# Attention values padded and packed in DRAM, the last normalisations on VectorE, and earlier filter tables in a four-layer attention and spectral kernel

## The chip, the cores and the metric

The kernel runs on one core of a Trainium2 chip. The metric is device microseconds from start to end of one execution. The kernel before takes 1390.59 us (median of 3 runs, 1387.26 to 1393.25).

## The reference, cut

Four sub-layers work on x, 2048 tokens of 576 values: sliding-window attention, a spectral filter, and both again with the same weights.

```python
def _A_ref(x, wqkv, wo):                 # H = 32 heads, Dh = 18, W = 256
    q, k, v = split of x @ wqkv by heads
    scores = jnp.einsum("bhqd,bhkd->bhqk", q, k) * (Dh ** -0.5)
    mask = (idx[:, None] - idx[None, :] >= 0) & (idx[:, None] - idx[None, :] < W)
    p = _softmax(jnp.where(mask, scores, -1e9), axis=-1)
    o = jnp.einsum("bhqk,bhkd->bhqd", p, v)
    return o.transpose(0, 2, 1, 3).reshape(B, S, D) @ wo

def _B_ref(x, w_r, w_i):
    X = rfft2(x) * (w_r + 1j * w_i)
    return irfft2(X, (S, D))

x = A_x
x = x + _A_ref(_layernorm(x), A_wqkv, A_wo)
x = x + _B_ref(_layernorm(x), B_w_r, B_w_i)
x = x + _A_ref(_layernorm(x), A_wqkv, A_wo)
x = x + _B_ref(_layernorm(x), B_w_r, B_w_i)
```

## The kernel before, in words

`layer_a` is an attention sub-layer, `layer_b` a spectral one. Between them stands the class `Out`, the output projection, whose units of 128 tokens run at once as the end of attention and the start of the spectral layer. TensorE (PE) multiplies, VectorE (DVE), ScalarE (ACT) and GpSimd (POOL) work on tiles, and nearly all transfers are issued by SP, in program order, from one list.

**Attention.** The 32 heads form eight groups (n = 0 to 7) of four. A group has 16 tiles of 128 queries, in four quarters (c) of 512. In a steady state TensorE mixes, in bursts, the work of several stages:

- `proj` (L1091) projects q and k of a later group; they go to DRAM (qk_d, L1126) and come back in a stacked layout by `stack_load` (L1132, 12 transfers of 18 partitions a quarter, L1141). `v_load` (L1144) brings v of a group, `vq` in the trace, 608 KB.
- `score_max` (L1154) multiplies q and k a first time (S, L1166) and VectorE takes each query's maximum (L1168).
- `m_rows` (L1176) turns a quarter's maxima (tile `mt`) and writes them with four small transfers (L1186) into a spare row of q, where k has ones.
- `exps` (L1191) multiplies a second time (E, L1203), now with the maximum subtracted. ScalarE exponentiates (L1204), POOL masks (L1206, L1209).
- `part` (L1214) multiplies by v (U, L1223). A column of ones in v gives the sums. After a quarter VectorE transposes the result (L1228, `us`).
- `divide` (L1236) inverts the sums on VectorE and multiplies on POOL (L1240; VectorE for the last quarter of all), `back` (L1242) transposes on VectorE into `o`, and `store` (L1246) issues four transfers, one a head: the tile has 32 partitions a head, of which 18 hold values, and L1250 stores 18 x 512 each to o_d in DRAM. Group 7's go straight to `out.o7` in SBUF.

The order of SP's list follows the order in which the Python code calls these functions. `bursts` (L1317) does it burst by burst; `later` (L1301) puts divide, back and store 1, 3 and 4 bursts after a quarter's last `part`. From MIX = 118 of 128 tiles a plain loop takes over. `behind` (L1389) interleaves the loads of the output projection: `attended` (L764) reads o_d (`oraw`, in two buffers big(0) and big(1)), `ahead_of_last` (L775) reads the last 56 features of o_d, and `turn` (L778) splits units into a high and a low part, where the subtraction for rows 64 to 127 (L785) is POOL's.

Transfers of SP run under eight semaphores in rotation, so a transfer is issued when the eighth before it has landed.

**Spectral layer.** `pre` (L218) is called once per unit n2 = 0 to 15 and loads the filter tables in eight transfers of 128 x 1024 (512 KB): four of `fc` at n2 = 2, 3, 10, 12 and four of `m2` at 5, 7, 11, 13. Tables 0 lie in big(0) and tables 1 in big(1), the buffers of `oraw`, whose units 0 to 7 and 8 to 15 must be done first. `f4` (L316) stores the units' result `ye` to yd in DRAM, and for the last ones also writes it to SBUF rows `ofree` (L337). In the second spectral layer 29 warm-up matmuls (L374) follow, then the phase `g0`, `g1m`, `g2` (L485 to L571), whose first matmuls (p, L501) read those rows and the tables.

The four transfers of the store:

```python
for h in range(4):
    to = o_d[72 * n + 18 * h:72 * n + 18 * h + 18, c] if n < NQ - 1 else out.o7[18 * h:18 * h + 18, 512 * c:512 * c + 512]
    (engines[h] if engines else nc.sync).dma_start(to, o[32 * h:32 * h + 18])
```

Of the kernel before, what the change touches and what calls it, by code (L numbers as in the profile page):

```python
# [8 lines left out]
F32 = mybir.dt.float32  # L9
# [6 lines left out]
S, D = 2048, 576  # L16
DF = 289
NF = 290
NT = 16
# [117 lines left out]
def layer_b(tc, xf, dst, dcs, gc, ident, rh, rl, big, out, ga_d, fc_d, m2_d, w_d, wo_d, wo2_d, dram, nxt, share):  # L137


    nc = tc.nc  # L140
    V, A, T, P = nc.vector, nc.scalar, nc.tensor, nc.gpsimd
    first = nxt is not None
# [5 lines left out]
    with ExitStack() as stack:  # L148
        banks, inner = ExitStack(), ExitStack()
        ip = stack.enter_context(tc.tile_pool(name="bi", bufs=1))  # L150
        cp = inner.enter_context(tc.tile_pool(name="bc", bufs=1))
# [22 lines left out]
        tables, ets = [], []  # L174
# [12 lines left out]
        for j in range(4):  # L187
            e = (ip if j == 1 else cp).tile([128, 2, 290], F32, name=f"eo{j}")
# [17 lines left out]
        def pre_o(j):  # L206
            nc.sync.dma_start(ws[j][:, 0:D], wo_d[:, j * D:j * D + D])

        def pre_w(k):

            w = wp.tile([128, 2, 2, NF], F32, tag="wt", name=f"wt{k}", bufs=NW)
            nc.sync.dma_start(w.rearrange("p a c f -> p a (c f)"), w_d[2 * k:2 * k + 2].rearrange("a p f -> p a f"))
            for q in range(2):
                wt[2 * k + q] = w[:, q]
# [2 lines left out]

        def pre(n2):  # L218

            if n2 in (2, 10):  # L220
                tables.append(big(n2 // 8, f"tables{n2 // 8}", F32).rearrange("p (w g x) -> p w g x", w=2, g=8))
            for w, d, at in ((0, fc_d, (2, 3, 10, 12)), (1, m2_d, (5, 7, 11, 13))):
                if n2 in at:
                    k = at.index(n2)
                    nc.sync.dma_start(tables[k // 2][:, w, 4 * (k % 2):4 * (k % 2) + 4].rearrange("p g x -> p (g x)"), d[:, 1024 * k:1024 * k + 1024])
            if n2 == 4:
                nc.sync.dma_start(edge[:, 0], fc_d[:, 4096:])
                nc.sync.dma_start(edge[:, 1], m2_d[:, 4096:])
            if n2 % 2 and n2 // 2 < NW:
                pre_w(n2 // 2)  # L230
            if first and n2 in (0, 3, 5, 8, 10):
                pre_o((0, 3, 5, 8, 10).index(n2))
# [83 lines left out]
        def f4(n2, h):  # L316
# [8 lines left out]
            else:  # L325
# [3 lines left out]
                V.tensor_sub(ye[:, 1], pz[:, 0, 0:NF], both[:, 0])  # L329
            yef = ye.rearrange("p j f -> p (j f)")  # L330
            pre(n2)
            if n2 == FD:
                for k in range(1 if first else 2):
# [60 lines left out]
        b = NT - 1  # L394
        if first:
# [24 lines left out]
            for t in range(1, NT - 5):  # L420
                u = t + 4
# [218 lines left out]
NQ = 8  # L640
# [73 lines left out]
class Out:  # L714
# [63 lines left out]
    def turn(self, u, e):  # L778

        raw = self.halves[u // 8].rearrange("p k c (n q) -> p k c n q", q=32)[:, :, :, u % 8]  # L780
        oT = self.oT[u % 3]
        h = oT[:, 0:512].rearrange("p (k c q) -> p k c q", k=4, c=4)
        (self.nc.vector.tensor_copy if e is self.nc.vector else self.nc.scalar.copy)(h, raw)  # L783
        self.nc.vector.tensor_sub(oT[:, 512:896].rearrange("p (k c q) -> p k c q", k=3, c=4), raw[:, 0:3], h[:, 0:3].bitcast(F32))
        self.nc.gpsimd.tensor_sub(h[64:128, 3], raw[64:128, 3], h[64:128, 3].bitcast(F32))  # L785

    def split_last(self, u):

# [73 lines left out]
def layer_a(tc, ident, eps, bp, big, src, dst, wqk_d, wv_d, wo_d, dc_d, gc_d, dram, copy, wvs, second, spectral, share):  # L862

    nc = tc.nc
    V, A, T, P = nc.vector, nc.scalar, nc.tensor, nc.gpsimd
# [2 lines left out]
    v_d = dram.tile([NQ, S, 76] if second else [NQ, 128, NT, 76], F32, name="v_d")  # L868

    o_d = dram.tile([504, 4, 512], F32, name="o_d")  # L870
    r_d = dram.tile([NQ, 4, 4, 512], F32, name="r_d")
    srcv, dstv = [a.rearrange("(p n) e -> p n e", n=NT) for a in (src, dst)]

    tiles = [slice(t * 128, (t + 1) * 128) for t in range(NT)]
# [5 lines left out]
    if True:  # L880
# [191 lines left out]
        with ExitStack() as c2:  # L1072
# [160 lines left out]

            os = {}

            def divide(n, c, drain=False):  # L1236
                u = us[n, c]
                rc = wp.tile([128, NT, 1], F32, tag="rc", name=f"rc{n}_{c}", bufs=2)
                V.reciprocal(rc, u[:, :, 18:19])
                (V if drain else P).tensor_mul(u[:, :, 0:18], u[:, :, 0:18], rc.to_broadcast([128, NT, 18]))  # L1240

            def back(n, c):  # L1242
                os[n, c] = o = wp.tile([128, NT, 32], F32, tag="o", name=f"o{n}_{c}", bufs=2)
                V.transpose(o, us[n, c])

            def store(n, c, engines=None):  # L1246
                o = os[n, c].rearrange("r n p -> r (n p)")
                for h in range(4):
                    to = o_d[72 * n + 18 * h:72 * n + 18 * h + 18, c] if n < NQ - 1 else out.o7[18 * h:18 * h + 18, 512 * c:512 * c + 512]
                    (engines[h] if engines else nc.sync).dma_start(to, o[32 * h:32 * h + 18])  # L1250

            for k, (i, c) in enumerate(((0, 0), (1, 0), (0, 1), (1, 1), (0, 2), (0, 3), (1, 2), (1, 3))):
                for f in proj(i, c, k % 2):
# [45 lines left out]
            steps = {}  # L1299

            def later(k, n, c):  # L1301
                for lag, f in zip(later.lags, (divide, back, store)):
                    steps.setdefault(k + lag, []).append((f, n, c))

            later.lags = 1, 3, 4

# [10 lines left out]
            def bursts():  # L1317
# [63 lines left out]
                for p in parts:  # L1381
                    part(*p)
                    if p[1] and p[0] % 4 == 3:
                        later(k, *divmod(p[0] // 4, 4))

            OB = NX - 8
            out = Out(nc, eps, bp, big, o_d, srcv, dstv, wo_d, dc_d, gc_d, second)

            def behind(t):  # L1389
                if copy and t >= 32 and t % 4 == 0 and t < 32 + 16 * len(copy):  # L1390

                    z, r = divmod(t // 4 - 8, 4)
                    P.dma_start(*[a[32 * r:32 * r + 32] for a in copy[z]])
                if t == OB - 16:
                    out.room()
                if 0 <= t - (OB - 10) < 10 and t % 2 == 0:
                    out.split((t - (OB - 10)) // 2)
                if t - OB + 13 in range(0, 10, 2):
                    out.const((t - OB + 13) // 2)
                if t == OB - 3:  # L1400
                    out.filters()
                if t - OB + 8 in range(0, 10, 2):
                    out.load_x(((t - OB + 8) // 2 + 1) % 5)
                if 0 <= t - (OB - 8) < 6:
                    out.attended(*divmod(t - (OB - 8), 2))
                if t - OB in (1, 2):
                    out.attended(3, t - OB - 1)
                if t == OB + 2:
                    out.ahead_of_last()
                if t - OB - 5 in (0, 1, 2):  # L1410
                    out.turn(t - OB - 5, V)
                if t == NX:

                    A.activation(wp.tile([128, 1], F32, name="se", bufs=1), eps, AF.Sqrt)
# [32 lines left out]
            def bank(tag, name):  # L1447
                return pp.tile([128, 512], F32, tag=tag, name=name, bufs=1 if tag == "pj" else 3)

            out.early(0, [bank(k, f"ops0_{k}") for k in ("pj", "S")], slice(0, 4))  # L1450
            divide(NQ - 1, 3, True)
            back(NQ - 1, 3)
            store(NQ - 1, 3, (nc.sync, nc.scalar, P, nc.sync))
            out.early(0, None, slice(4, 11))
# [56 lines left out]
```

## Time and profile before

| | before |
|---|---|
| median of 3 runs | 1390.59 us (1387.26 to 1393.25) |
| profiled execution, its time | 1393.43 us |
| its span | 1391.4 us |
| mean granted TensorE clock | 0.977 |
| first attention, stores of `o` | 160.9 us on |
| second attention, last store | about 1200 us |
| second spectral layer's warm-up | 1275.33 us |

The span runs from the first to the last instruction. In a timeline a row gives start, duration, engine, line, operation, output <- input, and in brackets how long the engine was idle before it and what ended that. SPq is SP's transfer queue at issue: the duration is that of issuing, not of the transfer. A row of the waits gives the engine and line, what was waited for, us in total, times and the longest. A row of the chain gives start, us and what the end waited for. A row of the windows gives the stretch, its length, busy time (and number of instructions) of PE, PE's weight loads, DVE, ACT and POOL, then the granted clock, the busy share of the 16 DMA engines and GB/s.

### The profile page before, as it was taken

The page shows a single profiled execution, that of the slowest core. Times are in us where ns is not written, and L with a number is a line of the kernel's source. Part 1 is how long each engine was busy: PE and PEld are TensorE (multiplying, and loading weights), DVE is VectorE, ACT ScalarE, POOL GpSimd, SP SyncE. Part 2 cuts the span into 40 slices and gives each one's busy share as a digit, 9 for nine tenths or more (in the row PEclk, how much of TensorE's full clock was granted, in tenths as well). Part 3 has the DMA queues.
Part 4 walks back from the last instruction along what each step waited for, and adds up shares of the span by engine and source line. Part 5 has one row for each costly group of instructions (what it writes and reads, how often), then busy time and mean ns, then how long its engine had stood idle before and what let it go on. Part 6 is the DMA issues. An engine that isn't in the chain of part 4 may idle for free.

```text
span 1391.4 us, 33481 instructions
## 1 busy us (share of the span) xinstructions
PE 1325.8 (95%) x10911; PEld 969.6 (70%) x10911; DVE 943.3 (68%) x3120; ACT 756.4 (54%) x1896; POOL 703.3 (51%) x1168
## 2 busy tenths in 40 slices
PE   9999999999998899999999999999999998998998
PEld 8986556556654499975999975565565554797588
DVE  5418878778887567757673168787788777475855
ACT  5623667567666735543355326676676667574233
POOL 2257556556655734467211395566566557312731
PEclk9999999999999999999999999999999999899999
DMA  6756555554445827678873467455455547488875
GB/s 199 210 168 200 180 169 161 166 170 155 149 143 172 228 72 246 188 247 264 274 246 77 117 200 214 148 163 156 147 155 145 164 130 247 105 291 283 290 242 180
DMA packets 175586, 259.56 MB, mean 187 GB/s; under 512 B 68639, under 2 KB 78623, under 8 KB 174981
## 3 DMA queue, kind: packets, MB, share of 16 engines
q1 hardware_dynamic: 164591, 236.04, 55.3%
q10 hardware_dynamic: 7702, 15.03, 3.1%
q0 software_dynamic: 3120, 6.36, 1.8%
q8 instruction: 88, 1.44, 0.4%
q14 instruction: 85, 0.70, 0.2%
HBM read 156.28 MB, written 100.13 MB: 184 GB/s over the span
## 4 chain that ended last, share of the span: by engine, by line
PE 77%; DMA 11%; DVE 3%; ACT 3%; issue 2%; SPq 2%; POOL 1%; DVEq 0%; ACTq 0%; POOLq 0%
PE pj L1105 18%; PE S L1166 11%; PE U L1223 10%; PE vps L1001 8%; PE ops L798 6%; PE E L1203 6%; DMA qs<-mt 4%; PE po L272 4%; PE p L501 3%; PE pq L522 3%; PE pi L598 2%; PE pf L272 2%; DMA ks<-qk_d 1%; ACT P L1204 1%; DMA qs<-qk_d 1%
## 5 line engine op out<-in xcount | busy, mean ns | idle before, releaser
L1168 DVE CUSTOM_DVE_ANT_0 jk<-S,mask 128x384 bf16<-128x384 f32 (+2 forms) x1024 | 490.3, 526 | 117.7 <-PE S L1166 71.7
L1204 ACT ACTIVATE P<-E 128x384 f32<-128x384 f32 (+2 forms) x1024 | 409.9, 476 | 222.8 <-PE E L1203 176.5
L1166 PE MATMUL S<-ks,qs 63*128 63x384 f32 (+2 forms) x1024 | 284.7, 381 | 1.4 <-DMA qs<-qk_d 0.4
L1206 POOL TENSOR_SCALAR_AFFINE_SELECT P<-P 128x512 f32<-128x512 f32 x256 | 163.3, 638 | 241.5 <-ACT P L1204 235.7
L1203 PE MATMUL E<-qs,ks 64*128 64x384 f32 (+2 forms) x1024 | 240.0, 386 | 36.8 <-DMA qs<-mt 31.7
L1166 PEld LDWEIGHTS S<-ks,qs 63*128 63x128 f32 x1024 | 147.7, 189 | 116.8 <-DVE m L1168 83.6
L1223 PE MATMUL U<-P,vq 128*19 128x128 f32 (+1 forms) x3840 | 197.7, 340 | 3.5 <-DVE us L1228 2.1
L1203 PEld LDWEIGHTS E<-qs,ks 64*128 64x128 f32 x1024 | 122.5, 192 | 61.3 <-issue 31.4
L1223 PEld LDWEIGHTS U<-P,vq 128*19 128x19 f32 x3840 | 98.1, 101 | 88.0 <-issue 27.5
L1105 PE MATMUL pj<-xh,wqh 128*128 128x512 f32 x360 | 158.2, 440 | 0.4 <-DVE sg L1123 0.2
L1209 POOL TENSOR_SCALAR_AFFINE_SELECT P<-P 128x512 f32<-128x512 f32 x224 | 143.3, 640 | 0.0
L1105 PE MATMUL pj<-xh,wql 128*128 128x512 f32 x360 | 122.5, 416 | 0.0
L1105 PE MATMUL pj<-xl,wqh 128*128 128x512 f32 x288 | 121.6, 422 | 0.0
L798 PE MATMUL ops<-oroom 128*128 128x290 f32 (+1 forms) x812 | 114.0, 297 | 1.7 <-DVE ofree L844 1.3
L798 PEld LDWEIGHTS ops<-oroom 128*128 128x128 f32 x812 | 110.4, 189 | 2.3 <-ACT ofree L832 1.5
L1105 PEld LDWEIGHTS pj<-xh,wqh 128*128 128x128 f32 x360 | 68.9, 191 | 33.4 <-issue 15.5
L1168 DVE DVE_READ_ACCUMULATOR2_ANT m<- 128x1 f32 x1024 | 85.5, 84 | 0.0
L1117 ACT CAST sg<-pj 128x512 fp32r<-128x512 f32 x72 | 42.4, 589 | 70.3 <-PE pj L1105 57.8
L1105 PEld LDWEIGHTS pj<-xh,wql 128*128 128x128 f32 x360 | 64.3, 189 | 21.8 <-issue 10.8
L1228 DVE STREAM_TRANSPOSE us<-U 128x512 f32<-128x512 f32 x64 | 45.9, 717 | 44.7 <-PE U L1223 44.7
L785 POOL TENSOR_TENSOR oroom<-oraw,oroom 64x128 fp32r<-64x128 f32 x32 | 17.7, 553 | 100.1 <-ACT oroom L783 56.9
L1105 PEld LDWEIGHTS pj<-xl,wqh 128*128 128x128 f32 x288 | 55.3, 192 | 17.1 <-issue 9.3
(507 smaller groups left out, 2258.1 us busy)
## 6 DMA issues: line engine op xcount, KB each, us to landing
qk_d<-sg SPq DMA_DIRECT2D x56, 512.0 KB
qs<-qk_d SPq DMA_DIRECT2D x384, 72.0 KB
ks<-qk_d SPq DMA_DIRECT2D x348, 72.0 KB
v_d<-vt SPq DMA_DIRECT2D x32, 304.0 KB
vq<-v_d SPq DMA_DIRECT2D x16, 608.0 KB
wt<-in_w SPq DMA_DIRECT2D x16, 580.0 KB
ofree<-x SPq DMA_DIRECT2D x16, 580.0 KB
x<-ofree SPq DMA_DIRECT2D x32, 290.0 KB
```

The costliest lines, as they stand in the source:

```text
L272: T.matmul(ps[:, c, 0:NF], tail[r] if si == 4 else hl_(si), dcs[b // 2][r, b % 2], start=mi == si == 0, stop=si == 4)
L798: self.nc.tensor.matmul(self.ps[u][n][:, 0:self.n], x, self.w[p][:, (2 * wk + n) * self.n:(2 * wk + n + 1) * self.n], start=first and i == ...
L1001: T.matmul(ps[:, n, 0:288], xT(xk, c), w[:, wk, n * 288:(n + 1) * 288], start=i == 0, stop=i == len(ks) - 1)
L1105: T.matmul(box["ps"].rearrange("r (n p) -> r n p", n=NT) if second else box["ps"], w[:, wk], x, start=s == 0, stop=s == len(ks) - 1)
L1166: T.matmul(ps[:, 0:N], q[b:b + 63, pair, i * 128:i * 128 + 128], k[b:b + 63, pair, lo:hi], start=True, stop=True)
L1168: V.tensor_tensor_reduce(out=jk[:, 0:N], in0=ps[:, 0:N], in1=mask[:, 384 - N:384], scale=1.0, scalar=-3e38, op0=ALU.add, op1=ALU.max, accu ...
L1203: T.matmul(ps[:, 0:nq], k[b:b + 64, pair, j * 128:j * 128 + 128], q[b:b + 64, pair, j * 128:j * 128 + nq], start=True, stop=True)
L1204: A.activation(p[:, hl_, 0:nq], ps[:, 0:nq], AF.Exp, scale=SC)
L1206: P.affine_select(out=p[:, :, 0:128], in_=p[:, :, 0:128], pattern=[[0, 4], [1, 128]], compare_op=ALU.is_ge, fill=0.0, base=0, channel_mult ...
L1209: P.affine_select(out=p[:, :, 256:384], in_=p[:, :, 256:384], pattern=[[0, 4], [-1, 128]], compare_op=ALU.is_gt, fill=0.0, base=0, channel ...
L1223: T.matmul(U[32 * h:32 * h + 19, (q0 % 4) * 128:(q0 % 4) * 128 + 128 * (q1 - q0)], vts[n][:, j, h], pt[n, j][:, h, (q0 - j) * 128:(q1 - j) ...
L1228: V.transpose(u, U.rearrange("r (p n) -> r n p", n=NT))
```

## The change

Five things:

1. For groups 0 to 6, `store` issues one transfer of the whole padded tile, 128 x 512, to a new DRAM buffer op_d (group, row, quarter), and no longer four.
2. A new function `pack` copies one head of a group, all four quarters, from op_d to o_d, as one DRAM-to-DRAM transfer of 16 rows of 2304 values (147 KB). `later` puts the four packs of a group 8, 10, 12 and 14 bursts after its last `part` (7, 7, 8, 8 for group 6). The trace's first pack of a group waits for the landing of its group's last store.
3. Group 7's multiplications in `divide` run on VectorE in all four quarters.
4. `turn`'s subtraction at L785 runs on VectorE for units 0 to 2; `ahead_of_last` is called two tiles later.
5. In the second spectral layer alone, tables 0 get a buffer of their own and load from n2 = 0, and tables 1 lie in big(0): fc at 0, 3, 6, 8 and m2 at 2, 5, 7, 10.

```diff
-            if n2 in (2, 10):
-                tables.append(big(n2 // 8, f"tables{n2 // 8}", F32).rearrange("p (w g x) -> p w g x", w=2, g=8))
-            for w, d, at in ((0, fc_d, (2, 3, 10, 12)), (1, m2_d, (5, 7, 11, 13))):
+            if n2 in ((2, 10) if first else (0, 6)):
+                k = len(tables)
+                t = big(k if first else 0, f"tables{k}", F32) if first or k else cp.tile([128, 2 * S], F32, name="tables0")
+                tables.append(t.rearrange("p (w g x) -> p w g x", w=2, g=8))
+            for w, d, at in ((0, fc_d, (2, 3, 10, 12) if first else (0, 3, 6, 8)), (1, m2_d, (5, 7, 11, 13) if first else (2, 5, 7, 10))):
...
-        self.nc.gpsimd.tensor_sub(h[64:128, 3], raw[64:128, 3], h[64:128, 3].bitcast(F32))
+        (self.nc.vector if u < 3 else self.nc.gpsimd).tensor_sub(h[64:128, 3], raw[64:128, 3], h[64:128, 3].bitcast(F32))
...
-                (V if drain else P).tensor_mul(u[:, :, 0:18], u[:, :, 0:18], rc.to_broadcast([128, NT, 18]))
+                (V if n == NQ - 1 else P).tensor_mul(u[:, :, 0:18], u[:, :, 0:18], rc.to_broadcast([128, NT, 18]))
...
                 o = os[n, c].rearrange("r n p -> r (n p)")
+                if n < NQ - 1:
+                    nc.sync.dma_start(op_d[n, :, c], o)
+                    return
                 for h in range(4):
-                    to = o_d[72 * n + 18 * h:72 * n + 18 * h + 18, c] if n < NQ - 1 else out.o7[18 * h:18 * h + 18, 512 * c:512 * c + 512]
-                    (engines[h] if engines else nc.sync).dma_start(to, o[32 * h:32 * h + 18])
+                    (engines[h] if engines else nc.sync).dma_start(out.o7[18 * h:18 * h + 18, 512 * c:512 * c + 512], o[32 * h:32 * h + 18])
+
+            def pack(n, h):
+                a, b = [f.rearrange("e c x -> (e c x)").rearrange("(a b) -> a b", a=16) for f in (o_d[72 * n + 18 * h:72 * n + 18 * h + 18], op_d[n, 32 * h:32 * h + 18])]
+                nc.sync.dma_start(a, b)
...
                     steps.setdefault(k + lag, []).append((f, n, c))
+                if c == 3:
+                    for h in range(4):
+                        steps.setdefault(k + (8 + 2 * h if n < NQ - 2 else 7 + h // 2), []).append((pack, n, h))
...
-                if t == OB + 2:
+                if t == OB + 4:
                     out.ahead_of_last()
```

SP's list in the second attention layer, around the first two quarters of a group, is this before (output <- input, shape, how many; the line number first; `mt_0` and `mt_1` are the maxima of quarters 0 and 1, `o_0` and `o_1` the values of quarters 0 and 1 of the group before):

```order
L1250 DMA o_d<-o_0_14203 18x512 x4
L892 DMA wqr_14281<-in_wqk 128x640
L1186 DMA qs_11657<-mt_0_14354 1x4x128 x4
L1126 DMA qk_d<-sg_2_14362 128x2x512
L1141 DMA qs_11656<-qk_d 18x2x512 x6
L1141 DMA ks_11658<-qk_d 18x2x512 x6
L1250 DMA o_d<-o_1_14450 18x512 x4
L1186 DMA qs_11657<-mt_1_14579 1x4x128 x4
```

The same stretch of SP's list now (line numbers shift by two, and L1251 is the padded store, L1258 the pack):

```order
L1258 DMA o_d<-op_d 16x2304
L1143 DMA qs_11601<-qk_d 18x2x512 x6
L1143 DMA ks_11603<-qk_d 18x2x512 x6
L1251 DMA op_d<-o_0_14128 128x512
L894 DMA wqr_14203<-in_wqk 128x640
L1258 DMA o_d<-op_d 16x2304
L1188 DMA qs_11601<-mt_0_14277 1x4x128 x4
L1258 DMA o_d<-op_d 16x2304
L1128 DMA qk_d<-sg_2_14285 128x2x512
L1143 DMA qs_11600<-qk_d 18x2x512 x6
L1143 DMA ks_11602<-qk_d 18x2x512 x6
L1258 DMA o_d<-op_d 16x2304
```

Ahead of the maxima's rows stands one store where there were four, and the four packs of the group before lie spread over this stretch. Ahead of quarters 2 and 3 stands one store and no pack.

At the end of the first attention layer SP's list before, from the last store of group 6 to the last maxima of group 7:

```order
L1250 DMA o_d<-o_3_7463 18x512 x4
L762 DMA ofree<-in_x 128x576
L770 DMA oraw_7326<-o_d 128x4x256
L758 DMA oroom<-gcr 128x512
L770 DMA oraw_7359<-o_d 128x4x256
L1186 DMA qs_1059<-mt_3_7570 1x4x128 x4
```

And now:

```order
L1251 DMA op_d<-o_3_7406 128x512
L764 DMA ofree<-in_x 128x576
L772 DMA oraw_7269<-o_d 128x4x256
L760 DMA oroom<-gcr 128x512
L772 DMA oraw_7302<-o_d 128x4x256
L1258 DMA o_d<-op_d 16x2304 x2
L1188 DMA qs_1059<-mt_3_7512 1x4x128 x4
L764 DMA ofree<-in_x 128x576
L1258 DMA o_d<-op_d 16x2304 x2
```

Two of the four packs of group 6 now stand between its last store and the last maxima's rows.

In the second spectral layer SP's list ahead of the rows for the next phase was:

```order
L823 DMA x_61<-ofree 128x580
L225 DMA tables_19268<-in_fc 128x1024
L337 DMA ofree<-ye_19387 8x580 x2
L340 DMA yd_18566<-ye_19387 16x8x580
L225 DMA tables_19268<-in_m 128x1024
L337 DMA ofree<-ye_19409 8x580
```

and is now:

```order
L825 DMA x_61<-ofree 128x580
L339 DMA ofree<-ye_19277 8x580 x2
L342 DMA yd_18454<-ye_19277 16x8x580
L339 DMA ofree<-ye_19297 8x580
```

The last table stands ten transfers earlier, right behind the store of an x unit. TensorE's and ScalarE's instructions and their order do not change; POOL gives 12 instructions to VectorE over the whole kernel.

More of the change, by code (lines that the diff above doesn't have):

```diff
@@ L870, in layer_a @@
     o_d = dram.tile([504, 4, 512], F32, name="o_d")
-    r_d = dram.tile([NQ, 4, 4, 512], F32, name="r_d")
+    op_d = dram.tile([NQ - 1, 128, 4, 512], F32, name="op_d")
     srcv, dstv = [a.rearrange("(p n) e -> p n e", n=NT) for a in (src, dst)]
@@ L1234, in layer_a, with divide @@
             os = {}
-            def divide(n, c, drain=False):
+            def divide(n, c):
                 u = us[n, c]
@@ L1450, in layer_a @@
             out.early(0, [bank(k, f"ops0_{k}") for k in ("pj", "S")], slice(0, 4))
-            divide(NQ - 1, 3, True)
+            divide(NQ - 1, 3)
             back(NQ - 1, 3)
```

## Prediction

> **What bounds the kernel now.** I read the page first, then the waits of the engines, then the timelines of TensorE and of SP's DMA queue around the longest waits, the chain, and the windows.
>
> ```profile
> PE 1325.8 (95%) x10911; PEld 969.6 (70%) x10911; DVE 943.3 (68%) x3120; ACT 756.4 (54%) x1896; POOL 703.3 (51%) x1168
> PE 77%; DMA 11%; DVE 3%; ACT 3%; issue 2%; SPq 2%; POOL 1%; DVEq 0%; ACTq 0%; POOLq 0%
> ```
>
> TensorE is busy for 95% of the 1391.4 us span and carries 77% of the chain. The diff leaves its instructions alone, so only what TensorE waits for, and the clock it is granted, can change. DMA's 11% is the target. What TensorE waits for in whole groups:
>
> ```profile
> PE E L1203 <- DMA qs<-mt: 31.7, 22, 3.3
> PE p L501 <- DMA ofree<-ye: 4.6, 1, 4.6
> PE U L1223 <- POOL P L1206: 1.3, 1, 1.3
> ```
>
> The first is the large one: the score matmul with the maximum already subtracted (E) waits for the four small row transfers (mt) that put the maxima into q's spare row. The longest of these waits, and others that the sum needs:
>
> ```profile
> 156.77 0.78 PE L1203 MATMUL E<-qs,ks 64*128 64x384 f32 x2 [1.18 <-DMA qs<-mt]
> 181.23 1.23 PE L1203 MATMUL E<-qs,ks 64*128 64x384 f32 x3 [2.56 <-DMA qs<-mt]
> 430.76 1.01 PE L1203 MATMUL E<-qs,ks 64*128 64x384 f32 x2 [2.68 <-DMA qs<-mt]
> 471.06 1.09 PE L1203 MATMUL E<-qs,ks 64*128 64x384 f32 x2 [2.65 <-DMA qs<-mt]
> 890.87 1.13 PE L1203 MATMUL E<-qs,ks 64*128 64x384 f32 x3 [3.27 <-DMA qs<-mt]
> 982.02 0.41 PE L1203 MATMUL E<-qs,ks 64*128 64x384 f32 x1 [2.63 <-DMA qs<-mt]
> 1180.86 1.13 PE L1203 MATMUL E<-qs,ks 64*128 64x384 f32 x2 [3.22 <-DMA qs<-mt]
> ```
>
> What SP issues before two of them (start, duration, count):
>
> ```profile
> 423.93 0.35 SPq L1149 DMA_DIRECT2D vq<-v_d  x1
> 424.42 1.96 SPq L1250 DMA_DIRECT2D o_d<-o  x4
> 426.82 3.81 SPq L1186 DMA_DIRECT2D qs<-mt  x4
> ...
> 977.26 2.90 SPq L1250 DMA_DIRECT2D o_d<-o  x4
> 980.25 2.44 SPq L1186 DMA_DIRECT2D qs<-mt  x4
> ```
>
> SP works without a pause at 977 to 983 us, and the four stores of 18 partitions stand directly ahead of the rows that TensorE needs: 2.90 us there, 1.96 us at 424. At 982 TensorE starts before SP's row is even over. At 426.82 the four rows take 3.81 us, 1.37 more than at 980: there SP itself is held until an earlier transfer has landed, and the one in question is the load of v just ahead.
>
> ```profile
> 980.25 1.63 DMA qs<-mt
> 1138.70 1.64 DMA qs<-mt
> ```
>
> In the chain the rows at 980 and 1139 end 1.6 us after the first was issued, before the fourth is even out: issue time and nothing else.
>
> **The stores and packs.** Per group and quarter, four stores become one, so three issues go. One issue costs between 0.305 us, the median, and a quarter of 2.90, 0.73 us:
>
> ```profile
> L1250 SPq DMA_DIRECT2D o_d<-o x224: 264/305/3399, 160.9 to 1172.7; - x112
> ```
>
> Three are worth 0.9 to 2.2 us. Each group's four packs give four issues back, and the new order puts them all between the last store of a group and the second store of the next: ahead of the first and of the second rows of a group stand one store and about two packs (one issue less than before), ahead of the third and fourth one store alone (three less). In each layer the first rows with stores ahead have no packs yet.
>
> Of the 31.7 us I strike what no store is ahead of, or what lies at the two ends of attention: 1.18, 2.65 and 3.22. 24.7 us in 19 waits are left. 181.23 and 890.87 (2.56 + 3.27 us, first rows with stores, no pack) are issue-bound and gain the full 0.9 to 2.2 each: take 1.8, together 3.6. 982.02 and its like stand behind two packs and one store: one issue, 0.3 to 0.7, so take 1.4 for two or three of them. The remaining 16 or so look like 430.76, where the load of v lands last. There the rows would be issued 1.5 us sooner, but come free only when that load is in; they gain 0 to 1.2 each, and I take 0.25, which is 4.0. Together **-9 us**. Low end: two times 0.9 and nothing else, -1.8; high end: 19 times 0.95, which is -18.
>
> Packs themselves: 147 KB from DRAM to DRAM, of which the trace of before has only one relative, issued by POOL (KB each, median us to landing):
>
> ```profile
> dcr<-in_dc POOLq DMA_DIRECT2D x4, 362.5 KB, 4.7
> ```
>
> It is 2.5 times as large. A pack should land in 2 to 4.7 us. Nobody needs it for tens of microseconds except in group 6. The first pack of a group reads what its group's last store wrote, and SP stands until that is in; the store is six issues ahead, four of them rows of mt (2.44 us), so some 2.8 us old. The nearest landing of a store is the 3.29 us of the row at 445.14 below, so SP stands about 0.5 us, and behind it wait the store and the rows of the next group. I take **+1 us** for all 14 of these waits (0 to +10, the latter if each holds TensorE 0.7 us).
>
> **The clock.** Waits of this length cost twice:
>
> ```profile
> 424.00:428.00 4.00, 4.00 (x54) 2.18 (x46) 4.00 (x16) 2.81 (x7) 3.33 (x5) 1.00 0.73 200
> 428.00:431.00 3.00, 0.32 (x3) 0.27 (x1) 0.66 (x4) 0.49 (x1) 1.23 (x2) 0.86 0.30 117
> 431.00:434.00 3.00, 3.00 (x22) 1.69 (x26) 2.06 (x8) 1.53 (x4) 0.00 (x0) 0.50 0.47 175
> 434.00:437.00 3.00, 3.00 (x27) 1.42 (x23) 1.82 (x10) 1.53 (x5) 1.86 (x3) 0.50 0.42 135
> ...
> 160.00:440.00 280.00, 267.42 (x2584) 161.97 (x2583) 222.25 (x858) 184.34 (x464) 164.75 (x241) 0.96 0.50 157
> 860.00:1150.00 290.00, 277.29 (x2663) 166.77 (x2663) 231.01 (x887) 190.20 (x479) 166.87 (x244) 0.97 0.51 152
> ```
>
> After the 2.68 us gap the granted clock is 0.50 for six microseconds, in which TensorE does 49 matmuls, 8.2 a microsecond, against 54 in the four full-speed microseconds ahead, 13.5; since the mixture differs I count the loss at a third of such a stretch. Over both attention stages 280 x 0.04 + 290 x 0.03 = 20 us of full clock are missing, so some 40 us run at half, and cost about 13. A wait that shrinks to about a microsecond leaves the clock alone (after the gap at 156.77 nothing of the kind is seen). Four waits of the larger size would be shortened enough: **-4 us** (0 to -10).
>
> The Trainium skill ("TensorE: Matmul & The Clock Gate", section "HAM oscillation — how this bites in real kernels") puts the limit at TensorE gaps over about 3.4 us. The trace disagrees: 2.68 us was enough here. By the page's rule this term would be nil and the forecast 4 us higher.
>
> **Ends of attention.** In each layer the rows of the very last quarter come to stand behind two packs of group 6, which read what that group's last store wrote, so that store must land first. The nearest row is a store of before:
>
> ```profile
> 445.14 3.29 DMA o_d<-o
> ```
>
> Before, the store was issued at 461.29 and the rows at 467.23:
>
> ```profile
> 461.29 1.62 SPq L1250 DMA_DIRECT2D o_d<-o  x4
> 467.23 2.54 SPq L1186 DMA_DIRECT2D qs<-mt  x4
> ```
>
> so a 3.3 us landing is over in time, and two more issues remain, 2 x 0.5 us (between 0.305 and 0.73): **+2 us** over the two layers, directly on TensorE's waits of 2.65 and 3.22 us (0 to +4).
>
> **VectorE for POOL.** The 1.34 us wait at the end of attention is POOL's:
>
> ```profile
> 485.55 0.76 POOL L785 TENSOR_TENSOR oroom<-oraw,oroom 64x128 fp32r<-64x128 f32 x1 [0.43 <-DVE oroom L783]
> 486.39 0.71 POOL L1206 TENSOR_SCALAR_AFFINE_SELECT P<-P 128x512 f32<-128x512 f32 x1
> 487.15 0.41 PE L1223 MATMUL U<-P,vq 128*19 128x128 f32 x8 [1.34 <-POOL P L1206]
> ```
>
> The subtraction of 0.76 us stands ahead of the mask; on VectorE it goes, and so does that wait: **-1.3 us** (0 to -2; VectorE takes over three multiplications and three subtractions a layer, and its 68% has room, but not exactly there).
>
> **Tables of the second spectral layer.** Four of eight loads of 512 KB are issued at 1264 to 1276, just ahead of the row that TensorE waits for before its next phase:
>
> ```profile
> 1275.68 0.58 SPq L225 DMA_DIRECT2D tables<-in_m  x1
> 1276.37 3.27 SPq L337 DMA_DIRECT2D ofree<-ye  x3
> ...
> 1278.33 5.25 DMA ofree<-ye
> ...
> 1283.93 1.24 PE L501 MATMUL p<-ofree,tables 128*64 128x290 f32 x4 [4.57 <-DMA ofree<-ye]
> ...
> 1218.00:1225.00 7.00, 5.73 (x43) 5.53 (x42) 4.58 (x14) 5.49 (x16) 0.58 (x1) 1.00 0.44 139
> 1240.00:1255.00 15.00, 15.00 (x114) 15.00 (x113) 11.36 (x31) 10.98 (x32) 2.35 (x4) 1.00 1.00 344
> 1275.00:1280.00 5.00, 4.36 (x31) 4.13 (x31) 1.46 (x4) 0.53 (x2) 4.69 (x9) 1.00 0.99 331
> ```
>
> The last 0.5 MB alone is 1.6 us at 331 GB/s, the last two 3.2 us, and both stand ahead of ye. Issued from the first step on, the 4 MB start at about 1212, where the DMA share is 0.4. The wait of 4.57 us goes but for about half a microsecond: **-4 us** (-1.5 for the last load alone, to -4.6). The price is more load in 1225 to 1255, where the share is 1.00 already, but TensorE is busy for all 15 us of 1240 to 1255, so its x arrives ahead of need.
>
> **The sum:** -9 - 4 + 1 + 2 - 1.3 - 4 = -15.3 us. The profiled execution took 1393.43 us, 2.0 more than its span and 2.84 above the median of 1390.59. So 1378.1 for an execution like it, and **1375.3** against the median.
>
> **Rivals.**
>
> Rows bound by the DMA queue (0.22). If landing and not issue decides everywhere, earlier issue gains only where the chain shows 1.6 us: -2.5, with -1 of clock, -1.3 and -3 for the tables, while the packs' and pads' bytes (some 256 KB a quarter, 0.75 us at 344 GB/s) cost +2 and the ends +1: -4.8, or **1386**. For it: the 3.81 at 426.82. Against: DMA shares of 0.50. The Trainium skill has a reason for it: "DMA: Bandwidth & Descriptors", section "Why a DMA increments its semaphore by 16 and not by 1", says that a transfer is dealt to the largest number of engines up to 16 that divides its outer dimension, so a store of 18 partitions uses nine and one of 128 sixteen, each with eight rows where four small ones gave eight to each of nine. No run here shows the number of engines.
>
> Packs hold SP (0.11): **slower**. SP goes on only when the transfer eight issues before is in. Eight issues take about 8 x 0.35 = 2.8 us, so a pack landing in 4.7 us, like dcr, stands SP for 1.9 us. 56 packs at 1.9 us and 0.3 of their own issue are 123 us of SP, against 168 store issues saved at 0.305 to 0.73, 51 to 123. At the low price SP loses 72 us; a quarter of that on TensorE's path (19 of the 56 quarters with a store ahead are waited for now, a third) is +18, less 6 for tables and subtraction, +12: **1403**. At that price SP breaks even at a landing of 2.8 - 0.3 + 51/56 = 3.4 us. Against it: a third of dcr's size, and a path not on POOL.
>
> Tables too early (0.07): the x loads of the first units queue behind 2 MB more, TensorE waits what it had gained, and 1379 is left.
>
> **How the numbers follow.** The forecast's own case has 0.60, and its bounds are 1363 (waits -18, clock -7) to 1384 (waits -1.8, tables -2.7). With the first rival's 1386 and its spread to 1392 the range 1363 to 1392 leaves out the slower case and a little on each side. 0.5% is 7 us, about what a measurement of this kernel can tell from no change: below 1383.6 is faster. That holds for the forecast's case but for 0.04 of it, for the table rival and for 0.04 of the first rival: 0.67. Same: the rest of both, and 0.01 of the slower case, 0.23; slower 0.10.
>
> **What would show it.** The profile after should have E's waits for mt at about 20 us instead of 31.7, the ones after 181 and 891 near 1 us, those behind v's load hardly changed; attention's granted clock 0.97 to 0.98; tail waits of 3 to 4 us; no wait for ye of over 1 us after the warm-up matmuls; no wait of U for POOL at the end of the first attention. I am wrong if SP's packs show 2 us and more each, if the mt waits stay at 30, or if TensorE waits for x at 1215 to 1260.

## The result and the profile after

The changed kernel takes 1371.37 us (median of 4 runs, 1368.36 to 1374.27) against 1391.23 us (the kernel before, now of 4 runs): a ratio of 0.9861, 95% interval 0.9826 to 0.9895, so 19 us less (15 to 24). The ratios here and below leave out two slow runs, one of the stores alone (1695.17 us, at a granted clock of 0.652) and one of the kernel before beside it (1398.99 us), which stand in the medians given. Forecast were 1375.3, and 15.3 less. Its profiled execution took 1368.36 us, with a span of 1366.3 us, 25.1 us shorter than the span before. It is the fastest of its four runs, and the profiled 1393.43 us of before are above all of its own, so the profiles show about 5 us more than the runs do.

The start of the page of after:

```profile
PE 1312.9 (96%) x10911; PEld 964.4 (71%) x10911; DVE 948.7 (69%) x3132; ACT 754.9 (55%) x1896; POOL 696.1 (51%) x1156
```

TensorE does the same instructions. Its waits, grouped, of after (total, times, longest):

```profile
PE E L1205 <- DMA qs<-mt: 22.2, 13, 3.4
PE p L503 <- DMA ofree<-yd: 1.7, 1, 1.7
```

The waits for the maxima's rows are 22.2 us in 13 times, and were 31.7 us in 22. The 4.6 us for ye are gone, and of the 1.3 us for POOL's mask 0.2 are left; a wait of 1.7 us for yd is new, later in the phase behind the warm-up, and so is one of 0.8 us for another of POOL's operations (L750). The granted clock in the two attention stages, the last columns but two of the windows of after:

```profile
160.00:440.00 280.00, 268.64 (x2624) 163.04 (x2616) 227.49 (x878) 187.34 (x475) 169.21 (x247) 0.99 0.59 186
860.00:1150.00 290.00, 279.78 (x2768) 167.65 (x2766) 240.57 (x928) 197.73 (x501) 174.51 (x253) 0.99 0.62 185
```

It was 0.96 and 0.97. In the same 280 us TensorE starts 2624 matmuls instead of 2584, and in 290 us 2768 instead of 2663, while the DMA engines carry more (0.59 and 0.62 instead of 0.50 and 0.51).

The place that the prediction showed at 424 us, in SP's timeline of after, eight microseconds earlier:

```profile
412.85 2.15 SPq L1143 DMA_DIRECT2D ks<-qk_d  x6
415.10 0.35 SPq L1151 DMA_DIRECT2D vq<-v_d  x1
415.90 0.34 SPq L1251 DMA_DIRECT2D op_d<-o  x1
416.63 2.46 SPq L1188 DMA_DIRECT2D qs<-mt  x4
```

The store takes 0.34 us where four took 1.96, and the four rows take 2.46 us instead of 3.81. TensorE's wait of 2.68 us at this place has gone. And the start of the second spectral layer's next phase, in TensorE's timeline of after:

```profile
1254.54 4.12 PE L376 MATMUL warm<-dc 128*128 128x290 f32 x29
1259.02 0.71 PE L503 MATMUL p<-ofree,tables 128*64 128x290 f32 x4 [0.36 <-issue]
...
1267.07 1.20 PE L503 MATMUL p<-ofree,tables 128*64 128x290 f32 x8 [1.74 <-DMA ofree<-yd]
```

From the first warm-up matmul to the first of the phase it is 4.48 us, and was 8.60 us.

Where the 25.1 us of the spans lie: warm-up starts 20.8 us sooner (1254.54 against 1275.33), which lies in attention and its ends; the warm-up's wait is worth 4.1 more; the remaining 0.2 is what is left after the new wait for yd and all else. How much of the 20.8 us is the change's and how much the chance of two executions, the next section tells.

### The profile page after: what moved, and what is told of

It reads as the page before. It is cut to its first block, busy times and chain, and to the rows that moved or that the text cites. A ratio compares the mean times of both kernels' runs of the same rounds, so it can differ in the third digit from the quotient of the medians.

```text
span 1366.3 us, 33335 instructions
## 1 busy us (share of the span) xinstructions
PE 1312.9 (96%) x10911; PEld 964.4 (71%) x10911; DVE 948.7 (69%) x3132; ACT 754.9 (55%) x1896; POOL 696.1 (51%) x1156
## 4 chain that ended last, share of the span: by engine, by line
PE 84%; DMA 7%; DVE 3%; ACT 3%; issue 2%; POOL 1%; SPq 1%; ACTq 0%; DVEq 0%; POOLq 0%
PE pj L1107 19%; PE S L1168 12%; PE U L1225 11%; PE vps L1003 9%; PE ops L800 6%; PE E L1205 6%; DMA qs<-mt 4%; PE po L274 4%; PE pq L524 3%; PE p L503 2%; PE pf L274 2%; PE pi L600 2%; PE pz L312 1%; ACT P L1206 1%; DMA dc<-dcr 1%
## 5 line engine op out<-in xcount | busy, mean ns | idle before, releaser
L1205 PE MATMUL E<-qs,ks 64*128 64x384 f32 (+2 forms) x1024 | 236.0, 381 | 29.0 <-DMA qs<-mt 22.2
L1225 PE MATMUL U<-P,vq 128*19 128x128 f32 (+1 forms) x3840 | 193.2, 334 | 3.3 <-DVE us L1230 2.2
L274 PE MATMUL po<-dc,half 128*128 128x290 f32 x384 | 63.4, 302 | 0.0
```

What stands on the lines that cost most here:

```text
L274: T.matmul(ps[:, c, 0:NF], tail[r] if si == 4 else hl_(si), dcs[b // 2][r, b % 2], start=mi == si == 0, stop=si == 4)
L1205: T.matmul(ps[:, 0:nq], k[b:b + 64, pair, j * 128:j * 128 + 128], q[b:b + 64, pair, j * 128:j * 128 + nq], start=True, stop=True)
L1225: T.matmul(U[32 * h:32 * h + 19, (q0 % 4) * 128:(q0 % 4) * 128 + 128 * (q1 - q0)], vts[n][:, j, h], pt[n, j][:, h, (q0 - j) * 128:(q1 - j) ...
```

## The experiments

The theory was that each part acts where the prediction put it, and that the stores act through the number of SP's issues. The rival was that it is the landing of transfers (fewer engines, bytes in the queue) that counts. All ratios are against the kernel before on the same chip; the kernel before took 1385.19, 1383.98 and 1382.38 us there. "Against the changed kernel" means the quotient with 0.9861.

**The parts alone.** The first keeps the kernel before, with the tables' part of the diff.

> The kernel before with only the earlier tables of the second spectral layer. My account: the wait of 4.57 us for ye after the warm-up matmuls goes, some 4 us less than before, 1387; nothing changes ahead of the second spectral layer. Rival (the loads only move the contention): a wait for another transfer of about the same size appears in the same phase, and the time stays within 1 us of 1391.

1378.96 us, ratio 0.9962 (0.9938 to 0.9986): 5.3 us less, 2 to 9. TensorE's timeline of this run:

```profile
1265.91 0.72 PE L503 MATMUL p<-ofree,tables 128*64 128x290 f32 x4 [0.42 <-issue]
```

The wait for ye is gone; one of 1.6 us for yd a little later is new. The account holds. The waits of TensorE and of SP show besides how far attention differs from one execution to the next, since this kernel's attention is that of before:

```profile
PE E L1205 <- DMA qs<-mt: 24.5, 19, 4.5
...
SPq L1188 <- DMA vq<-v_d: 6.7, 6, 1.7
```

24.5 us here against 31.7: a sum of these waits is good to some 7 us, and the granted clock of a stage to 0.02. The warm-up starts at 1261.5 us here, 13.8 us sooner than in the profile of before, with the same attention. So two executions differ that much without the stores, much of the 20.8 us above can be chance, and sizes have to come from the ratios.

The second is the changed kernel with the parts for tables, multiplications and subtractions taken back.

> The kernel before with only the padded stores and the packs (and the read of the last features two tiles later); tables, multiplications and subtractions as before. My account: TensorE's waits for mt come to 20 to 24 us instead of 31.7, fewer microseconds at half clock, and 12 to 15 us less than before, 1376 to 1379. Rival (much of the gain in the profile was the luck of one execution with few half-clock stretches): 5 to 8 us less, 1383 to 1386.

1367.21 us, ratio 0.9877 (0.9832 to 0.9921): 17 us less, 11 to 23. Its waits:

```profile
PE E L1203 <- DMA qs<-mt: 15.3, 12, 2.6
PE p L501 <- DMA ofree<-ye: 3.3, 1, 3.3
```

15.3 us of waits for mt, against 24.5 to 32.0 in the three traces with the old attention. This part carries nearly the whole gain, and more than the 10 us that I gave it.

The third is the kernel before with `V if n == NQ - 1 else P` in divide and `self.nc.vector if u < 3` in turn.

> The kernel before with only the multiplications of the last group and the subtractions of units 0 to 2 on VectorE. My account: the wait of 1.34 us for POOL's mask at the end of the first attention goes and nothing else, 1.3 us less. Rival (VectorE is itself late at the end of attention): a wait for VectorE's results takes its place, 0 to 2 us more than before.

1384.17 us, ratio 0.9993 (0.9967 to 1.0018): -1.0 us, between -4.6 and +2.5. Its trace has at the place of the 1.34 us:

```profile
482.31 0.41 PE L1223 MATMUL U<-P,vq 128*19 128x128 f32 x8 [0.17 <-POOL P L1206]
```

The wait went; a microsecond is less than the runs can tell. The three ratios together give 0.9833, the same as the 0.9861 of all at once within the intervals.

**Issue or landing.** The same bytes to the same places, with four issues again:

```diff
-                    nc.sync.dma_start(op_d[n, :, c], o)
+                    for h in range(4):
+                        nc.sync.dma_start(op_d[n, 32 * h:32 * h + 32, c], o[32 * h:32 * h + 32])
```

> The changed kernel with the padded store issued as four transfers of 32 partitions, the same bytes to the same places. Issue account (mine): four issues stand ahead of mt again and the packs come on top, waits for mt at 28 to 40 us, 8 to 20 us slower than the changed kernel, 1379 to 1391. Landing account (one transfer over all 128 partitions lands sooner, the number of issues does not matter): waits for mt stay near 22 us, within 4 us of the changed kernel, 1368 to 1375.

1427.3 us, ratio 1.0301 (1.026 to 1.0343): 61 us more than the changed kernel, three times the upper end of what the issue account expected, and 3% slower than the kernel before. 168 issues more cost 0.36 us each; part of it comes by the granted clock, 0.966 over its six runs where the changed kernel's four have 0.985. Its waits, and SP's and TensorE's timelines where the load of v stands ahead:

```profile
PE E L1205 <- DMA qs<-mt: 55.3, 30, 5.2
```

```profile
436.12 2.15 SPq L1143 DMA_DIRECT2D ks<-qk_d  x6
438.37 0.35 SPq L1151 DMA_DIRECT2D vq<-v_d  x1
438.82 1.77 SPq L1252 DMA_DIRECT2D op_d<-o  x4
440.69 3.78 SPq L1188 DMA_DIRECT2D qs<-mt  x4
...
444.93 1.02 PE L1205 MATMUL E<-qs,ks 64*128 64x384 f32 x2 [4.02 <-DMA qs<-mt]
```

The four rows take 3.78 us again, as before the change. With four stores between them, the fourth row is the eighth transfer after the load of v, and SP issues a transfer only when the eighth before it has landed; with one store the eighth before it is a load of k, which did not hold it: in the changed kernel the four rows take 2.46 us. SP's own waits at the rows show the same. Of this run:

```profile
SPq L1188 <- DMA vq<-v_d: 8.8, 6, 2.0
```

and of the kernel before:

```profile
SPq L1186 <- DMA vq<-v_d: 5.6, 6, 1.6
```

The two other kernels with four stores have 6.7 and 9.0 us of it; in the changed kernel and the nine others with one store it does not occur at all. The landing account falls: the number of transfers matters. Whether it acts by the time of issuing or by the place in the rotation, this run does not separate; SP's waits for vq at the rows, 8.8 us, are the smaller share of its 61 us.

**What an issue costs anywhere.** A second pack behind each, to a buffer that nobody reads:

```diff
                 nc.sync.dma_start(a, b)
+                nc.sync.dma_start(spare_d[72 * n + 18 * h:72 * n + 18 * h + 18].rearrange("e c x -> (e c x)").rearrange("(a b) -> a b", a=16), b)
```

> The changed kernel with every pack issued twice, the second time to a DRAM buffer that nobody reads: 56 more issues of 0.526 us, 29 us of SP, and 8 MB more to move. SP-full account (in attention SP's list is as long as TensorE's work, so each issue costs its time): 8 to 20 us slower than the changed kernel. Wait-by-wait account (the prediction's: only what stands directly ahead of a waited-for mt counts): 2 to 6 us slower, the waits for mt growing only where a pack stands ahead of quarters 0 and 1.

1400.3 us, ratio 1.011 (1.0087 to 1.0133): 35 us more than the changed kernel, above both accounts, far above the wait-by-wait one. TensorE's waits for the rows are nearly twice the 22.2 us of the changed kernel:

```profile
PE E L1206 <- DMA qs<-mt: 42.4, 21, 6.1
```

Since a second pack moves bytes too, the next run issues a transfer of 512 bytes in its place:

```diff
+                nc.sync.dma_start(spare_d[4 * n + h, 0:1, 0:128], op_d[n, 32 * h:32 * h + 1, 0, 0:128])
```

> The changed kernel with one more SP transfer behind every pack, of 512 bytes only, from op_d to a DRAM buffer that nobody reads: 56 more issues and no bytes to speak of. The doubled packs cost some 34 us; this tells issue from bytes. Issue account (SP-full): 12 to 34 us slower than the changed kernel. Bytes account (the doubled packs' 8 MB held up other transfers): within 4 us of it.

1388.13 us, ratio 1.0027 (1.0005 to 1.0048): 23 us more than the changed kernel for 56 issues without bytes, 0.41 us each. The rows for it and for the waits:

```profile
L1260 SPq DMA_DIRECT2D spare_d<-op_d x56: 473/587/1625, 197.9 to 1182.5; - x56
...
PE E L1206 <- DMA qs<-mt: 33.0, 21, 4.6
```

So seven tenths of the issue's median 0.587 us reach the end of the kernel. (An added transfer also moves the rotation on by one; the run does not tell the two apart.) The other way round, the bytes without SP's issues:

```diff
+                P.dma_start(spare_d[72 * n + 18 * h:72 * n + 18 * h + 18].rearrange("e c x -> (e c x)").rearrange("(a b) -> a b", a=16), b)
```

> The changed kernel with every pack issued a second time, to a DRAM buffer that nobody reads, by POOL instead of SP: the bytes of the doubled packs without SP's issues. Issue account (SP-full): within 5 us of the changed kernel, the 5 for POOL's own issues ahead of masks. Bytes account: 15 to 34 us slower, as the doubled packs on SP.

1382.92 us, ratio 0.9997 (0.9976 to 1.0019): 19 us more than the changed kernel, which by the number is what the bytes account expected. The waits tell another cause:

```profile
PE U L1226 <- POOL P L1209: 19.7, 14, 2.9
PE E L1206 <- DMA qs<-mt: 13.6, 11, 1.9
...
POOL spare_d L1260 <- DMA qs<-mt: 27.6, 5, 6.9
```

The 8 MB show no sign of having held up the rows: the waits for mt are shorter than the 22.2 us of the changed kernel, though a TensorE that waits for POOL also gives SP time. What is late is POOL, which stands at these transfers (27.6 us for mt alone) with the masks queued behind. Why 56 second packs on SP cost 11 us more than 56 small transfers is not settled: bytes may have a part in it there.

**Taking waits off SP.** In the changed kernel SP still stands at two places of attention (SP's waits of after):

```profile
SPq L1143 <- DMA qk_d<-sg: 60.7, 35, 9.5
SPq L1258 <- DMA op_d<-o: 20.2, 10, 3.4
```

The first kernel moves the packs (`10 + 2 * h` for `8 + 2 * h`):

> The changed kernel with the packs of groups 0 to 5 two bursts later (10, 12, 14, 16), so that the group's last store has landed by the time of its first pack. SP's wait for op_d, 20.2 us in 10 times, goes. SP-full account: 2 to 6 us faster than the changed kernel. Wait-by-wait account (the prediction gave all of these waits 1 us): within 1.5 us of it.

1361.99 us, ratio 0.984 (0.9808 to 0.9873): 3 us less than the changed kernel, give or take 7. Of this run:

```profile
PE E L1205 <- DMA qs<-mt: 20.4, 14, 4.1
...
SPq L1258 <- DMA op_d<-o: 5.6, 2, 3.0
```

What is left of SP's wait for op_d fits the packs of group 6, which were not moved, once in each layer. TensorE's waits for mt are 20.4 us, hardly shorter, and the time cannot be told from no change. The second moves the stacked loads (`divmod(t + 16, NT)` for `t + 20` in `loads`):

> The changed kernel with the stacked q and k of groups 2 to 7 loaded four tiles later (16 tiles instead of 20 ahead), in the same order on SP. In the changed kernel SP stands 60.7 us in 35 times at these loads until qk_d has landed, with mt queued behind. SP-full account: most of these waits inside attention go, 3 to 8 us faster. Rival (the loads then come too late for the first score matmul, S): a wait of S for qs or ks appears, 0 to 10 us slower.

1360.42 us, ratio 0.9836 (0.9807 to 0.9865): 3.5 us less, again within the uncertainty, with waits for mt at 12.1 us. SP's waits for qk_d did not go, as the account has it: 48.8 us in 25 times are left of 60.7 in 35. Some waits of S, the rival's sign, appear; the row names a store, but S reads only q and k (of this run):

```profile
PE E L1205 <- DMA qs<-mt: 12.1, 9, 3.3
PE S L1168 <- DMA op_d<-o: 5.6, 2, 3.5
```

Both together:

> The changed kernel with both the packs two bursts later and the stacked q and k loaded four tiles later. SP-full account: SP's waits for op_d and half of those for qk_d go, TensorE's waits for mt under 12 us, 6 to 10 us faster than the changed kernel. Rival (each of the two only moved SP's waiting to the other place): no faster than either alone, 2 to 4 us.

1357.85 us, ratio 0.981 (0.9776 to 0.9844): 7 us less than the changed kernel, 0.5 to 14; waits for mt 9.9 us. SP's waits for qk_d are 52.8 us in 32 times, so only the op_d half of the SP-full account's sign is there, and the interval leaves the rival's 2 to 4 us open. With the packs of groups 0 to 5 on POOL besides (`(P if n < NQ - 2 else nc.sync).dma_start(a, b)`):

> The same as the one before, with the packs of groups 0 to 5 issued by POOL instead of SP: 48 issues of 0.53 us go from SP. SP-full account: 5 to 12 us faster still. Rival (a pack's issue on POOL stands ahead of the masks that TensorE's U matmuls wait for, or waits itself for the eighth transfer before): waits of U for POOL of 3 us and more, 0 to 10 us slower than the one before.

1351.82 us, ratio 0.9758 (0.9728 to 0.9789): 6 us less still than the kernel without POOL's packs, on the same chip, give or take 6, and 14 us less than the changed kernel, which is clear of noise. It beats both kernels. Its waits:

```profile
PE E L1205 <- DMA qs<-mt: 6.7, 4, 2.7
PE S L1168 <- DMA ks<-qk_d: 3.0, 1, 3.0
```

Of the rival's waits of U for POOL there are 0.3 us, against 19.7 with the second packs. A likely reason, not tested by itself, is that the packs come two bursts later here, when the store has landed.

**An attempt that failed.** Two of each quarter's four rows issued by ScalarE:

```diff
-                        (nc.sync if n or c > 1 else nc.scalar).dma_start(
+                        (nc.sync if (n or c > 1) and hp == 0 else nc.scalar).dma_start(
```

> The changed kernel with two of the four mt transfers of every quarter issued by ScalarE instead of SP: SP loses two issues of 0.579 us a quarter, some 65 us in all, ScalarE gains them. SP-full account: waits for mt under 10 us instead of 22.2, 6 to 14 us faster than the changed kernel. Rival (ScalarE's exponentials come later by the issues, and TensorE or POOL waits for them): waits for P at E or U grow by as much, 0 to 10 us slower.

1505.68 us, ratio 1.089 (1.0847 to 1.0932): 143 us more than the changed kernel, against both accounts. SP's waits and its timeline:

```profile
SPq L1143 <- DMA qs<-mt: 135.4, 55, 5.4
```

```profile
309.24 2.28 SPq L1143 DMA_DIRECT2D qs<-qk_d  x6
311.98 5.90 SPq L1143 DMA_DIRECT2D ks<-qk_d  x6
```

ScalarE issues its two rows in the middle of that:

```profile
314.33 1.20 ACTq L1188 DMA_DIRECT2D qs<-mt  x2
```

SP now stands at its loads, 5.90 us for six where 2.15 is usual, until rows have landed that ScalarE issues. My reading is that the two engines share the eight semaphores in rotation, so that the order in the code ties SP's eighth transfer after a row to that row's landing; the waits fit it, the semaphores themselves were not read. The rival's sign came as well:

```profile
PE E L1205 <- ACT P L1206: 34.5, 33, 8.2
```

In the changed kernel these are 6.5 us in 13 times. The relief of SP was more than undone, so the run says nothing on the theory.

## Why the prediction was right, and where not

The time, the range and the direction were right, and the parts lie where they were put; how the gain of the stores comes about was right only in part. Point by point:

- **Tables, -4.** Right: 4.1 us in the profile, 5.3 (2 to 9) alone. The extra load in the stretch of full DMA share cost TensorE nothing that shows; the third rival did not come.
- **VectorE for POOL, -1.3.** The wait went, in the changed kernel as by itself. The size is below what runs can tell.
- **Ends of attention, +2.** Not seen: the two waits of 2.65 and 3.22 us became 2.23 and 3.42, together 0.2 less. From the turned maxima to the first of the rows it does take SP 3.78 and 4.48 us instead of 2.89 and 2.88, but the end of attention absorbs it.
- **Stores, packs, clock and ends together, -10.** The direction was right and the size too small: 17 us (11 to 23) alone, of which some 5 or 6 are the clock's by the bullet on it below. The step that failed is "the remaining 16 or so look like 430.76 ... but come free only when that load is in; they gain 0 to 1.2 each, and I take 0.25". The prediction had seen that SP is held there until v has landed, and took it that the rows stay bound to that landing. They do not: the fourth row is the eighth transfer behind v's load only with four stores in between, and one store takes that coincidence away. 2.68 us at 430.76 went altogether, and SP's wait for vq at the rows, there in all four traces with four stores, is in none with one. Twelve waits of before have a load of v just ahead of the store and come to 14.2 us; after there are five, of 6.2 us in all, so 8 us went where the sum had 4.0. SP's hold explains only part of that: it is six waits of 5.6 us, all in the first attention layer.
- **First rows, and rows behind packs.** The first rows without packs gained 2.7 us by the profile, 3.6 were forecast (2.56 and 3.27 became 0.97 and 2.15). The other waits inside attention, with no load of v ahead, grew from 4.6 to 7.2 us, where 1.4 less was forecast for the stalls behind packs (2.63 at 982.02 became 2.76 at 969.28). That all waits for mt together came out 9.5 us shorter, with 9 forecast, is therefore luck, the more so as such a sum is good to 7 us. The chain's 1.6 us at 980 are not "issue time and nothing else" either: TensorE waits first for the first of the four rows, whose issue takes 0.573 us (median), so by my estimate some 1.1 us are its landing.
- **Counting only what stands directly ahead.** The whole of the pricing went wait by wait. In attention SP's list is nearly as long as TensorE's work: SP's rows of the timeline add up to 266 of the 290 us from 860 to 1150 in the kernel before, in which TensorE is busy for 277, and to 251 in the changed kernel, in both cases with SP's standing inside them. So a transfer added costs about as much as its issue, 0.36 to 0.62 us each in three runs, also where it does not stand directly ahead of mt.
- **First packs, +1.** I had SP stand 0.5 us at the first pack of a group; it stands 2.0 (20.2 us in 10 times). The packs two bursts later save 3 us, give or take 7, which does not tell 1 us from 4.
- **The clock, -4.** Right in size, by the clocks of the runs. The five runs of the stores alone have a mean granted clock of 0.986, the 22 of the kernel before beside them 0.980. These 0.006 are 8 us of full clock, 16 us at half, and by the prediction's own third 5 or 6 us. The two profiles say more than that (0.96 and 0.97 to 0.99, and TensorE busy for 12.9 us less with the same instructions), but with the attention of before TensorE is busy for 1316.7 and 1318.1 us in two other profiles, and for 1315.7 with the stores alone, so about half of the 12.9 can be chance. No run changes the clock without the waits that go with it.

The trigger of the clock term is borne out only in part. In the changed kernel a wait of 1.99 us ends at 1122.28, in TensorE's timeline and the windows around it, and one of 2.76 us at 969.28:

```profile
1122.28 1.01 PE L1205 MATMUL E<-qs,ks 64*128 64x384 f32 x2 [1.99 <-DMA qs<-mt]
...
1116.00:1120.00 4.00, 4.00 (x54) 2.18 (x52) 4.00 (x16) 3.01 (x8) 3.56 (x5) 1.00 1.12 206
1122.00:1125.00 3.00, 2.72 (x18) 1.94 (x18) 1.55 (x5) 0.94 (x3) 0.15 (x1) 0.50 0.71 227
1125.00:1128.00 3.00, 3.00 (x27) 1.42 (x23) 1.86 (x9) 1.53 (x5) 1.86 (x3) 0.50 0.52 140
```

```profile
969.28 0.41 PE L1205 MATMUL E<-qs,ks 64*128 64x384 f32 x1 [2.76 <-DMA qs<-mt]
...
969.00:972.00 3.00, 2.72 (x14) 1.79 (x15) 1.78 (x8) 1.03 (x3) 0.69 (x2) 1.00 0.19 66
972.00:975.00 3.00, 3.00 (x32) 1.73 (x31) 2.63 (x11) 2.15 (x7) 1.23 (x2) 1.00 0.46 145
```

Six microseconds at 0.50 follow the wait of 1.99 us, and the longer one of 2.76 us leaves the clock at 1.00. So the length of a wait alone does not decide, and that a wait has to shrink "to about a microsecond" is more than the traces say; what else decides stays open. The limit of about 3.4 us in the Trainium skill ("TensorE: Matmul & The Clock Gate", section "HAM oscillation — how this bites in real kernels") is not borne out by this trace either: 1.99 us was enough.

The first rival, rows bound by the DMA queue, is refuted as it was put, landing and not issue everywhere: the same bytes in four transfers cost 61 us, and with 8 MB more from POOL the waits for mt did not grow. The reason that the Trainium skill offered for it ("DMA: Bandwidth & Descriptors", section "Why a DMA increments its semaphore by 16 and not by 1") would give transfers of 32 partitions all sixteen engines, as it does the one of 128; they were the slowest form all the same. No trace here shows the engines of one transfer.

The second rival, packs that hold SP, did not come in its form. Its break-even was a landing of 3.4 us, and the only packs whose landing a trace shows are POOL's. Its second packs take 3.7 us, and its packs in the fastest kernel above 3.9:

```profile
DMA to landing us min/median/max: 2.4/3.7/6.2
```

Those of SP, whose landing no trace gives, hardly ever held it. SP's timeline of after shows how late the eighth transfer behind a pack comes:

```profile
957.70 0.53 SPq L1258 DMA_DIRECT2D o_d<-op_d  x1
958.34 0.51 SPq L1128 DMA_DIRECT2D qk_d<-sg  x1
958.95 2.44 SPq L1143 DMA_DIRECT2D qs<-qk_d  x6
961.44 4.05 SPq L1143 DMA_DIRECT2D ks<-qk_d  x6
```

It is the first load of k, 3.7 us after the pack, where the rival had reckoned 2.8. SP's waits name a pack that has not landed just once, for 0.2 us. Its other half, that SP's time passes to TensorE, was nearer the truth than my own pricing: with four stores and the packs the kernel is slower than before.

## What to carry to other kernels

Where one queue issues nearly all transfers, add up its list for one period of the steady state and set it beside the bound engine's period, before pricing single waits: if the two are close, every issue added or taken off can count, also one that stands ahead of nothing urgent. Count transfers before bytes (here 56 transfers of 512 bytes cost 23 us and 56 of 144 KB 35 us), and look at which transfer is the eighth ahead (or whatever the rotation is) of the urgent one: a large load in that place holds the urgent transfer's issue, and one transfer more or less moves it out. Before moving a transfer to another engine, see whether the two share a rotation: by the reading above, that ties the two engines together.

## What the runs showed of the hardware that was not expected

A DRAM-to-DRAM transfer of 144 KB issued by POOL lands in 3.7 us (median, 2.4 to 6.2) as a second pack and in 3.9 us in the fastest kernel here, not much less than the 4.7 us of one of 362.5 KB. A transfer of 512 bytes takes SP as long to issue (0.587 us, median) as a second pack of 144 KB (0.587 us). The granted clock halved after a wait of TensorE of 1.99 us and did not after one of 2.76 us.
